# Attention loop with one normalised tile of h per iteration; k's weights over two queues and in halves; v's first product with its low weights last

## The chip, the cores and the metric

The kernel runs on one core of one Trainium2 chip. The metric is the device time of one execution in microseconds (us); of several executions the median is given. One execution was also recorded by the hardware profiler. Its rows are called the profile or the trace here, and times inside it count from the start of the recorded span.

## The reference

The input x is 2048 tokens by 512 channels in float32. First comes attention with a learned feature map, then an MLP that mixes tokens:

```python
h  = x + A(_layernorm(x))
h2 = h + B(_layernorm(h))
# A, for 32 heads of width 16:
q, k, v = split(x @ wqkv)
pq, pk  = q @ w_phi, k @ w_phi                       # per head
phi_q = concat([softmax(pq), softmax(-pq)])          # likewise phi_k
kv, z = phi_k^T v, sum over tokens of phi_k
o  = (phi_q kv) / (phi_q . z + 1e-6);   A = o @ wo
# B, over the token axis, 2048 -> 1792 -> 2048:
u  = gelu(h^T w1 + b1);   B = (u w2 + b2)^T
```

## The kernel before

The 2048 tokens are 16 tiles of 128. Products run on TensorE in a float32 format that takes 128 columns of weights at a time; to keep precision, an operand is split into a high part (a rounded copy, made by ScalarE) and a low part (the difference, made by VectorE or GpSimd). `mm3` (lines 63 to 67) makes of each product three: high by high (L65), high by low (L66), low by high (L67). `split` (L58) makes the two parts.

The engines are called as in the profile: PE (TensorE), PEld (its weight load), ACT (ScalarE), DVE (VectorE), POOL (GpSimd), SP (SyncE, which here only issues DMAs). Each takes its instructions in the order written.

**Start (lines 223 to 362).** Nine products of `ones` (L291 to L293) keep PE at work while the first weights arrive. The transposed weights come in chunks of 128 rows by 512 columns (`load_w`, L228): chunks 4 to 7 are k's, 8 to 11 v's, 0 to 3 q's. All chunks are issued by SP, in the order of the lines 235 to 252, mixed with the tiles of x. Each chunk is centred (`center`, L257: on DVE with a sum, a small multiply and an add of the mean; or on ACT with two passes), folded with the feature map or transposed into PSUM (`fold`, L269), copied out as high weights (`hi_w`, L281) and subtracted to low weights (`lo_w`, L287). For each tile t of x, `split_x` (L109) makes X[t] in two parts, the high one on ACT (L60), the low one on POOL (L61). `proj` (L122) multiplies X[t] with weights; with `by_part` its products stand in an order that lets k's first product begin before all weights are there. From line 294 to line 356 the order of PE, DVE, ACT and POOL is written out by hand; what follows until line 422 (the rest of k, v, and some tiles of q) is ordered by a scheduler. v's first product `v0` (L335) writes into a PSUM buffer of the pool `ps_v` (two buffers), which the folds of chunks 10 and 11 hold until `lo_w` has read them.

**Attention loop (lines 423 to 704).** Again the order on PE, DVE, ACT and POOL is written out by hand. Iteration `it` (L648) works on several tiles at once:

- POOL: `s_pq(it+1)` scales the query features (L465), `s_ez(it+3)` multiplies by z (L447), `s_rstd(it-3)` makes the reciprocal deviation r2 by a power (L590) and multiplies it into the mean (L591), and the low part of the normalised tile is made by L61. In the first iterations `negate` (L160) stands among them.
- PE: `s_num` (L551, even iterations, for two tiles), `q_mm` as long as there are tiles of q, `fills` (L642, up to two tiles of the MLP's first product, L65 to L67 into `pu`), `s_wo(it-2)` (L564, into `po`) and `s_tr(it)` (transposes, L532). `s_num` and `s_tr` share the one PSUM buffer `tn`.
- ACT: copies out of `tn` (`pht`, L534; `oh`, L557), the exponentials (L176), the moments of a tile of h (L585 to L587), the normalised tile `hn` (L595) and its high part (L60), and the high part `whi` of the MLP weights (L614).
- DVE: the denominators (L456 to L462), sums (L221), `ol` (L562), the low part `wlo` of the MLP weights (L606, queued in `LATER` and written by `flush`, L603), and `s_h` (L575), which adds x to the attention's output and frees `po` (one buffer) for the next `s_wo`.

A tile of h thus goes through: `s_wo` and `s_h` in iteration t+2; moments and `s_rstd` in t+3; `s_hn` (L593). In the kernel before, `s_hn` runs only in even iterations, for two tiles: tile it-4 near the beginning (L663), tile it-3 at the end (L697), right behind its own `s_rstd`. The first product of the MLP takes tile it-5 in iteration it (L645).

**MLP (from line 715).** The rest of the first product, gelu, and the second product in a seven-product scheme. The change leaves these lines as they are.

Of the kernel before, what the change touches and what calls it, by code (L numbers as in the profile page):

```python
# [12 lines left out]
ALU = mybir.AluOpType  # L13
# [23 lines left out]
def block_kernel(ctx: ExitStack, tc: tile.TileContext, x, xT, wT, phic, wo, w1, b1, w2, b2,  # L37
# [13 lines left out]
    eps2 = cst.tile([P, 1], F32, name="eps2")  # L51
    r2 = cst.tile([P, NT], F32, name="r2")
    cst.tile([P, 80], F32, name="pad")
    nc.vector.memset(ones, 1.0)
    nc.vector.memset(mhalf, -0.5)
    nc.vector.memset(eps2, EPS * EPS)

# [61 lines left out]
        nc.vector.tensor_scalar(ve, st[:, 1:2], 1.0 / D, EPS, op0=ALU.mult, op1=ALU.add)  # L119
        nc.gpsimd.tensor_tensor(r1[:, t:t + 1], ve, mhalf[:, :1], op=ALU.pow)  # L120

    def proj(t, wh, wl, pool, name, by_part=False):  # L122
        o = pool.tile([P, D], F32, name=name, tag=name)
        if by_part:
            half, whole = [slice(0, D // 2), slice(D // 2, D)], slice(0, D)
            turn = [(0, wh, half[0]), (0, wh, half[1]), (1, wh, whole), (0, wl, half[0]), (0, wl, half[1])]
            for i, (a, w, cols) in enumerate(turn):
                for kt in range(KD):
                    nc.tensor.matmul(o[:, cols], X[t][:, a, kt, :], w[:, kt, cols], start=i == 0 and kt == 0,
                                     stop=i >= 3 and kt == KD - 1, skip_group_check=True)  # L130
            return o
        for kt in range(KD):
            mm3(o, X[t][:, 0, kt, :], X[t][:, 1, kt, :], wh[:, kt, :], wl[:, kt, :],
                kt == 0, kt == KD - 1)
        return o
# [87 lines left out]
    with tc.tile_pool(name="prep", bufs=1) as prep:  # L223
        pc = prep.tile([P, 72], F32, name="pc")
        ph = prep.tile([P, 4, P], F32, name="ph")
        WR = {}

        def load_w(c):  # L228
            if c % 2 == 0:
                pair = big.tile([P, 2, D], F32, name="wraw2", tag="big")  # L230
                WR[c], WR[c + 1] = pair[:, 0], pair[:, 1]
            nc.sync.dma_start(WR[c], wT[c * P:(c + 1) * P, :])

        nc.scalar.dma_start(pc, phic)
        for c in range(4, 8):
            load_w(c)
        xr = {0: load_x(0), 1: load_x(1)}
        nc.sync.dma_start(ident, ident_in)
        for c in range(8, 12):
            load_w(c)  # L240
        xr[2] = load_x(2)
        load_h(0)
        load_h(1)
        xr[3] = load_x(3)
        for c in range(4):
            load_w(c)
        load_h(2)
        xr[4] = load_x(4)
        load_h(3)
        nc.sync.dma_start(mask, kvmask)  # L250
        nc.sync.dma_start(b1s, b1)
        nc.sync.dma_start(b2s, b2)

        FO = {}
        HL = {0: (wqh, wql), 1: (wkh, wkl), 2: (wvh, wvl)}

        def center(c, vector):  # L257

            mu = prep.tile([P, 1], F32, name="mu", bufs=3)
            if vector:  # L260
                nc.vector.reduce_sum(mu, WR[c], axis=AX.X)
                nc.vector.tensor_scalar_mul(mu, mu, -1.0 / D)
                nc.vector.tensor_scalar(WR[c], WR[c], mu, None, op0=ALU.add)
            else:
                junk = prep.tile([P, D], F32, name="junk")
                nc.scalar.activation(junk, WR[c], AF.Copy, scale=-1.0 / D, accum_out=mu)
                nc.scalar.activation(WR[c], WR[c], AF.Identity, bias=mu)

        def fold(c, pool, name):  # L269
            FO[c] = pool.tile([P, KD, P], F32, name=name, tag=name)  # L270
            for kt in range(KD):
                if c < 8:
                    nc.tensor.matmul(FO[c][:, kt, :], WR[c][:, kt * P:(kt + 1) * P], ph[:, c % 4, :],
                                     start=True, stop=True)
                else:
                    nc.tensor.transpose(FO[c][:, kt, :], WR[c][:, kt * P:(kt + 1) * P], ident)

        def parts(c):
            return [w[:, :, c % 4 * P:(c % 4 + 1) * P] for w in HL[c // 4]]

        def hi_w(c, vector=False):  # L281
            if vector:
                nc.vector.tensor_copy(parts(c)[0], FO[c])
            else:
                nc.scalar.activation(parts(c)[0], FO[c], AF.Copy)

        def lo_w(c):  # L287
            hi, lo = parts(c)
            nc.vector.tensor_sub(lo, FO[c], hi)

        warm = ps_k.tile([P, P], F32, name="pk_ps", tag="pk_ps")  # L291
        for _ in range(WARM):
            nc.tensor.matmul(warm, ones, ones, start=True, stop=True)  # L293
        with tc.manual_schedule(engines={ET.PE, ET.DVE, ET.Activation, ET.Pool}):

            nc.gpsimd.tensor_mul(ph.rearrange("p c (a f) -> p c a f", f=DH),
                                 pc[:, 0:64].rearrange("p (c f) -> p c f", f=DH).unsqueeze(2).to_broadcast([P, 4, 8, DH]),
                                 pc[:, 64:72].unsqueeze(1).unsqueeze(3).to_broadcast([P, 4, 8, DH]))
            center(4, True)
            center(5, False)  # L300
            fold(4, ps_q, "pu")
            center(6, True)
            fold(5, ps_q, "pu")
            center(7, False)
            fold(6, ps_v, "pv")
            fold(7, ps_v, "pv")
            hi_w(4, True)
            hi_w(5, True)
            hi_w(6, True)
            split_x(0, xr[0])  # L310
            hi_w(7)
            for c in range(4, 8):
                lo_w(c)
            split_x(1, xr[1])
            k0 = proj(0, wkh, wkl, ps_k, "pk_ps", True)
            center(8, True)
            for c in range(9, 12):
                center(c, False)
            k1 = proj(1, wkh, wkl, ps_k, "pk_ps")
            for c in range(8, 12):  # L320
                fold(c, *((ps_q, "pu"), (ps_v, "pv"))[c // 10])
            k_ops(0, k0)
            split_x(2, xr[2])
            k_ops(1, k1)
            stats_x(0)
            k2 = proj(2, wkh, wkl, ps_k, "pk_ps")
            for c in range(8, 12):
                hi_w(c)
            for c in range(8, 12):
                lo_w(c)  # L330
            stats_x(1)
            exps(0, PK[0])
            split_x(3, xr[3])
            split_x(4, xr[4])
            v0 = proj(0, wvh, wvl, ps_v, "pv")  # L335
            k_ops(2, k2)
            stats_x(2)
            k3 = proj(3, wkh, wkl, ps_k, "pk_ps")
            k_norm(0)
            center(0, True)  # L340
            v_out(0, v0)
# [12 lines left out]
            lo_w(0)  # L354
            lo_w(1)
            center(3, False)
        stats_x(3)
        exps(3, PK[3])
        for c in range(2, 4):
            fold(c, ps_q, "pu")  # L360
            hi_w(c)
            lo_w(c)
# [225 lines left out]

    def s_rstd(t):
        nc.gpsimd.tensor_tensor(r2[:, t:t + 1], VE[t][:, 0:1], mhalf[:, :1], op=ALU.pow)  # L590
        nc.gpsimd.tensor_mul(VE[t][:, 1:2], VE[t][:, 1:2], r2[:, t:t + 1])  # L591

    def s_hn(t):  # L593
        hn = ak.tile([P, D], F32, name="hn")
        nc.scalar.activation(hn, HT[t], AF.Identity, scale=r2[:, t:t + 1], bias=VE[t][:, 1:2])  # L595
        HN[t] = big.tile([P, 2, D], F32R, name="hs", tag="big")
        split(HN[t][:, 0], HN[t][:, 1], hn, nc.gpsimd)
# [47 lines left out]
        if FN[0] <= it - LAG:  # L645
            fill(0, ps_f)

    for it in range(NT + 3):  # L648
        even = it % 2 == 0
        if 0 <= it + 1 < NT:  # L650
            s_pq(it + 1)
# [3 lines left out]
        if it == 1:  # L655
            run(q_logits(0))
            q_mm()
            s_tr(1)
        if it > 1 and even:
            if it <= NT:  # L660
                s_num(it // 2 - 1)
            if it >= 4:
                s_hn(it - 4)  # L663
        den = s_den(it + 2) if it + 2 < NT else []
        if it > 1 and even and it <= NT:
            ol = s_ol(it // 2 - 1)
# [8 lines left out]
        fills(it)  # L675
        q_exp(0)
        logits = q_logits(1)
        if it >= 3 and even:
            s_moments(it - 3)
        if it > 1 and even and it - 2 < NT:  # L680
            s_wo(it - 2)
# [1 line left out]
            s_tr(it)  # L683
        if it > 1 and not even and it - 2 < NT:
            s_wo(it - 2)
        if it >= 3 and not even:
            s_moments(it - 3)
        if it >= 3:
            s_rstd(it - 3)
        run(logits + (q_sums(0) if it > 0 else []), den)  # L690
        flush()
        if 0 <= it - 2 < NT:
            s_h(it - 2)
        if it > 0:
            negate()
        if it >= 3 and even:
            s_hn(it - 3)  # L697
        for p in range(2):
            if it >= LAG - 3 + p and FL[p] <= FN[p] + 2 * (FN[p] > 0):
                fill_load(p)  # L700
# [259 lines left out]
```

## Time and profile before

| what | value |
|---|---|
| time, median of 3 runs | 528.55 us (527.94 to 528.89) |
| the profiled execution's own time | 527.88 us |
| its span | 526.1 us |
| mean granted TensorE clock | 0.999 |
| busy: PE, DVE, ACT, POOL | 516.9, 394.0, 277.7, 245.2 us |

The span is what the instructions cover; the execution takes 1.78 us more. The rows that follow in the prediction are of three kinds. A timeline row gives start, duration, engine, line, operation and tiles; in brackets behind it stands how long the engine was idle before it and who ended that. A group row (of the costliest groups) gives all instructions of one line and shape: busy time, mean of one in ns, and the idle time before them with its releaser. A row of the windows gives, for a stretch of time, the busy time of each engine with the number of its instructions. The end of a matmul is modelled, and neighbours overlap in the pipeline, so distances between starts say more than durations: undisturbed, one matmul of 512 columns starts every 0.23 us.

### The profile page before, as it was taken

The page shows a single profiled execution, that of the slowest core. Times are in us where ns is not written, and L with a number is a line of the kernel's source. Part 1 is how long each engine was busy: PE and PEld are TensorE (multiplying, and loading weights), DVE is VectorE, ACT ScalarE, POOL GpSimd, SP SyncE. Part 2 cuts the span into 40 slices and gives each one's busy share as a digit, 9 for nine tenths or more (in the row PEclk, how much of TensorE's full clock was granted, in tenths as well). Part 3 has the DMA queues.
Part 4 walks back from the last instruction along what each step waited for, and adds up shares of the span by engine and source line. Part 5 has one row for each costly group of instructions (what it writes and reads, how often), then busy time and mean ns, then how long its engine had stood idle before and what let it go on. Part 6 is the DMA issues. An engine that isn't in the chain of part 4 may idle for free.

```text
span 526.1 us, 8910 instructions
## 1 busy us (share of the span) xinstructions
PE 516.9 (98%) x3379; PEld 436.5 (83%) x3379; DVE 394.0 (75%) x681; ACT 277.7 (53%) x480; POOL 245.2 (47%) x204
## 2 busy tenths in 40 slices
PE   9999999999999979999999999999999999999997
PEld 8888888887877757777788888888889999999997
DVE  6893999976899989874426423824869889888985
ACT  6999843534247676557757422625553424444430
POOL 2589699985999988897425000000002122211210
PEclk9999999999999999999999999999999999999999
DMA  8634210020122233334234345532114686667733
GB/s 307 205 120 121 83 40 21 1 87 17 56 86 80 82 103 118 104 119 130 91 101 120 92 143 169 175 104 82 60 61 109 161 191 150 137 153 190 162 44 78
DMA packets 36298, 58.52 MB, mean 111 GB/s; under 512 B 3744, under 2 KB 19360, under 8 KB 36256
## 3 DMA queue, kind: packets, MB, share of 16 engines
q1 hardware_dynamic: 31936, 51.37, 30.4%
q0 software_dynamic: 4032, 6.42, 8.8%
q8 instruction: 26, 0.43, 0.3%
q10 hardware_dynamic: 288, 0.17, 0.1%
q14 instruction: 16, 0.13, 0.1%
HBM read 46.81 MB, written 11.14 MB: 110 GB/s over the span
## 4 chain that ended last, share of the span: by engine, by line
PE 82%; POOL 12%; DVE 3%; ACT 2%; issue 0%; POOLq 0%; ACTq 0%
PE py L822 11%; PE pu L65 11%; PE pu L66 10%; PE pu L67 10%; PE py L826 10%; PE py L823 6%; POOL ez L447 4%; POOL eq L465 3%; PE pv L66 3%; PE pv L67 3%; PE pv L65 3%; PE pk_ps L65 2%; PE pk_ps L66 2%; PE pk_ps L67 2%; POOL hs L61 2%; PE kvp L212 2%
## 5 line engine op out<-in xcount | busy, mean ns | idle before, releaser
L606 DVE TENSOR_TENSOR wlo<-wraw,whi 128x512 fp32r<-128x512 f32 x56 | 50.9, 912 | 56.2 <-ACT whi L614 56.0
L65 PE MATMUL pu<-hs,whi 128*128 128x512 f32 x224 | 87.2, 395 | 0.0
L66 PE MATMUL pu<-hs,whi 128*128 128x512 f32 x224 | 87.1, 389 | 0.0
L67 PE MATMUL pu<-hs,wlo 128*128 128x512 f32 x224 | 87.1, 390 | 0.0
L881 POOL DMA_DIRECT2D out<-ot x7 | 6.2, 889 | 157.3 <-DVE ot L877 157.3
L795 ACT ACTIVATE whi<-wraw 128x1792 fp32r<-128x1792 f32 x28 | 47.5, 1701 | 46.6 <-PE py L822 20.6
L804 DVE TENSOR_TENSOR wlo<-wraw,whi 128x1792 fp32r<-128x1792 f32 x28 | 56.5, 2022 | 12.5 <-PE py L823 8.9
L822 PE MATMUL py<-uf,whi 128*128 128x512 f32 x175 | 63.4, 399 | 0.0
L614 ACT ACTIVATE whi<-wraw 128x512 fp32r<-128x512 f32 x56 | 34.9, 626 | 50.3 <-PE pu L66 46.0
L65 PEld LDWEIGHTS pu<-hs,whi 128*128 128x128 f32 x224 | 42.1, 188 | 10.8 <-issue 2.5
L67 PEld LDWEIGHTS pu<-hs,wlo 128*128 128x128 f32 x224 | 42.1, 188 | 9.0 <-DVE wlo L606 0.4
L823 PE MATMUL py<-uf,wlo 128*128 128x256 f32 x175 | 49.2, 281 | 0.0
L66 PEld LDWEIGHTS pu<-hs,whi 128*128 128x128 f32 x224 | 42.1, 188 | 8.5
L447 POOL TENSOR_TENSOR ez<-eq,zB 128x1024 f32<-128x1024 f32 x16 | 40.6, 2539 | 4.4 <-ACT zB L494 4.4
L826 PE MATMUL py<-uf,whi 128*128 128x256 f32 x210 | 39.0, 283 | 0.0
L822 PEld LDWEIGHTS py<-uf,whi 128*128 128x128 f32 x175 | 33.0, 188 | 6.8
L200 POOL TENSOR_TENSOR pk<-pk,sk 128x1024 f32<-128x1024 f32 x16 | 31.0, 1940 | 7.6 <-DVE sk L199 5.0
L826 PEld LDWEIGHTS py<-uf,whi 128*128 128x128 f32 x210 | 32.4, 189 | 1.4
L823 PEld LDWEIGHTS py<-uf,wlo 128*128 128x128 f32 x175 | 33.1, 189 | 0.0
L465 POOL TENSOR_TENSOR eq<-eq,w 128x1024 f32<-128x1024 f32 x16 | 31.9, 1996 | 1.2 <-DVE w L462 1.2
L204 POOL TENSOR_TENSOR zacc<-zacc,pk 128x1024 f32<-128x1024 f32 x13 | 31.2, 2402 | 0.5
L61 POOL TENSOR_TENSOR hs<-hn,hs 128x512 fp32r<-128x512 f32 x16 | 21.4, 1340 | 17.9 <-ACT hs L60 17.9
(179 smaller groups left out, 1329.2 us busy)
## 6 DMA issues: line engine op xcount, KB each, us to landing
wraw<-in_w SPq DMA_DIRECT2D x56, 256.0 KB, 2.8
wraw<-in_w SPq DMA_DIRECT2D x28, 512.0 KB, 4.1
xraw<-in_xT SPq DMA_DIRECT2D x16, 256.0 KB, 2.9
xh<-in_x SPq DMA_DIRECT2D x16, 256.0 KB, 2.6
h<-in_x SPq DMA_DIRECT2D x16, 256.0 KB, 2.7
out<-h SPq DMA_DIRECT2D x16, 256.0 KB, 3.0
out<-ot POOLq DMA_DIRECT2D x14, 256.0 KB, 4.5
wraw<-in_wT SPq DMA_DIRECT2D x12, 256.0 KB, 4.9
```

The costliest lines, as they stand in the source:

```text
L65: nc.tensor.matmul(o, ah, bh, start=first, stop=False)
L66: nc.tensor.matmul(o, ah, bl, start=False, stop=False)
L67: nc.tensor.matmul(o, al, bh, start=False, stop=last)
L447: nc.gpsimd.tensor_mul(EZ[t], EQ[t], zB)
L465: nc.gpsimd.tensor_mul(heads(EQ[t]), heads(EQ[t]), W[t].rearrange("p g c h -> p (g c h)").unsqueeze(2).to_broadcast([P, 2 * H, DH]))
L606: LO.append(nc.vector.tensor_sub(wl_, raw, wh_).ins)
L614: nc.scalar.activation(wh_, raw, AF.Copy)
L795: nc.scalar.activation(WH[g], RAW[g], AF.Copy)
L804: nc.vector.tensor_sub(wl_, RAW[g], WH[g])
L822: nc.tensor.matmul(o, a[0], b, start=start, stop=stop, skip_group_check=True)
L823: nc.tensor.matmul(o[:, 0], a[1], b[:, 0], start=False, stop=stop, skip_group_check=True)
L826: nc.tensor.matmul(o[:, half], a[x], b[:, y], start=start and first and i == 0, stop=stop and i == 2, skip_group_check=True)
```

## The change

Three groups of edits. (1) At the start, `ones` is set by POOL; chunks 5 and 7 are issued by ACT's queue instead of SP's; chunks 4 and 7 are centred in two halves of 256 columns, and chunk 7's high weights are copied in two halves. (2) v's low weights are made in the order 10, 11, 8, 9, and v0 multiplies with all high weights first and with the low weights in its last four products. (3) In the attention loop, `s_hn(it-4)` runs once in every iteration, behind the exponentials and ahead of the moments; the loop has one iteration more; r2 is multiplied into the mean by ACT ahead of `hn` and no longer by POOL; and where logits are still made in the iteration, `s_h` stands ahead of `flush`.

```diff
-    nc.vector.memset(ones, 1.0)
+    nc.gpsimd.memset(ones, 1.0)
...
-    def proj(t, wh, wl, pool, name, by_part=False):
+    def proj(t, wh, wl, pool, name, by_part=False, low_last=False):
...
+            if low_last:
+                turn = [(0, wh, whole), (1, wh, whole), (0, wl, whole)]
...
-            nc.sync.dma_start(WR[c], wT[c * P:(c + 1) * P, :])
+            (nc.scalar if c in (5, 7) else nc.sync).dma_start(WR[c], wT[c * P:(c + 1) * P, :])
...
-        def center(c, vector):
+        def center(c, vector, parts=1):
...
-                nc.vector.tensor_scalar(WR[c], WR[c], mu, None, op0=ALU.add)
+                for part in range(parts):
+                    cols = slice(part * D // parts, (part + 1) * D // parts)
+                    nc.vector.tensor_scalar(WR[c][:, cols], WR[c][:, cols], mu, None, op0=ALU.add)
...
-        def hi_w(c, vector=False):
+        def hi_w(c, vector=False, parts_of=1):
...
-                nc.scalar.activation(parts(c)[0], FO[c], AF.Copy)
+                for k in range(0, KD, KD // parts_of):
+                    kts = slice(k, k + KD // parts_of)
+                    nc.scalar.activation(parts(c)[0][:, kts], FO[c][:, kts], AF.Copy)
...
-            center(4, True)
+            center(4, True, 2)
-            center(7, False)
+            center(7, False, 2)
-            hi_w(7)
+            hi_w(7, parts_of=2)
...
-            for c in range(8, 12):
+            for c in (10, 11, 8, 9):
                 lo_w(c)
...
-            v0 = proj(0, wvh, wvl, ps_v, "pv")
+            v0 = proj(0, wvh, wvl, ps_v, "pv", low_last=True)
...
     def s_rstd(t):
         nc.gpsimd.tensor_tensor(r2[:, t:t + 1], VE[t][:, 0:1], mhalf[:, :1], op=ALU.pow)
-        nc.gpsimd.tensor_mul(VE[t][:, 1:2], VE[t][:, 1:2], r2[:, t:t + 1])
     def s_hn(t):
+        nc.scalar.activation(VE[t][:, 1:2], VE[t][:, 1:2], AF.Copy, scale=r2[:, t:t + 1])
...
-    for it in range(NT + 3):
+    for it in range(NT + 4):
...
-        if it > 1 and even:
-            if it <= NT:
-                s_num(it // 2 - 1)
-            if it >= 4:
-                s_hn(it - 4)
+        if it > 1 and even and it <= NT:
+            s_num(it // 2 - 1)
...
         logits = q_logits(1)
-        if it >= 3 and even:
+        if it >= 4 and even:
+            s_hn(it - 4)
+        if 3 <= it < NT + 3 and even:
             s_moments(it - 3)
...
-        if it >= 3 and not even:
+        if it >= 4 and not even:
+            s_hn(it - 4)
+        if 3 <= it < NT + 3 and not even:
             s_moments(it - 3)
-        if it >= 3:
+        if 3 <= it < NT + 3:
             s_rstd(it - 3)
         run(logits + (q_sums(0) if it > 0 else []), den)
-        flush()
+        if it > 0:
+            negate()
+        if not logits:
+            flush()
         if 0 <= it - 2 < NT:
             s_h(it - 2)
-        if it > 0:
-            negate()
-        if it >= 3 and even:
-            s_hn(it - 3)
+        flush()
```

More of the change, by code (lines that the diff above doesn't have):

```diff
@@ L120, in stats_x @@
         nc.gpsimd.tensor_tensor(r1[:, t:t + 1], ve, mhalf[:, :1], op=ALU.pow)
-    def proj(t, wh, wl, pool, name, by_part=False):
+    def proj(t, wh, wl, pool, name, by_part=False, low_last=False):
         o = pool.tile([P, D], F32, name=name, tag=name)
-        if by_part:
+        if by_part or low_last:
             half, whole = [slice(0, D // 2), slice(D // 2, D)], slice(0, D)
             turn = [(0, wh, half[0]), (0, wh, half[1]), (1, wh, whole), (0, wl, half[0]), (0, wl, half[1])]
+            if low_last:
+                turn = [(0, wh, whole), (1, wh, whole), (0, wl, whole)]
             for i, (a, w, cols) in enumerate(turn):
@@ L129, in proj @@
                     nc.tensor.matmul(o[:, cols], X[t][:, a, kt, :], w[:, kt, cols], start=i == 0 and kt == 0,
-                                     stop=i >= 3 and kt == KD - 1, skip_group_check=True)
+                                     stop=w is wl and kt == KD - 1, skip_group_check=True)
             return o
@@ L266, in center @@
                 nc.scalar.activation(junk, WR[c], AF.Copy, scale=-1.0 / D, accum_out=mu)
-                nc.scalar.activation(WR[c], WR[c], AF.Identity, bias=mu)
+                for part in range(parts):
+                    cols = slice(part * D // parts, (part + 1) * D // parts)
+                    nc.scalar.activation(WR[c][:, cols], WR[c][:, cols], AF.Identity, bias=mu)
         def fold(c, pool, name):
```

## The prediction

> **What bounds the kernel now.** I read the busy times first, then who ends PE's waits, then the timeline of PE, POOL, ACT and DVE around these waits, and the groups of POOL's instructions in the same stretch.
>
> ```profile
> PE 516.9 (98%) x3379; PEld 436.5 (83%) x3379; DVE 394.0 (75%) x681; ACT 277.7 (53%) x480; POOL 245.2 (47%) x204
> ```
>
> PE is busy for 516.9 of 526.1 us and the change takes no product away. What can be won is PE's lost time, some 9 us, and only the part that the edits touch. Among PE's waits those for `pht`, at `s_num` (L551), are the largest; their rows show where they sit:
>
> ```profile
> 194.84 1.10 PE L551 MATMUL tn<-pht,kvB 64*32 64x256 f32 x32 [2.77 <-ACT pht L534]
> ...
> 208.81 1.10 PE L551 MATMUL tn<-pht,kvB 64*32 64x256 f32 x32
> ...
> 220.84 0.50 PE L65 MATMUL po<-woh,oh 128*128 128x512 f32 x1 [0.76 <-DVE h L579]
> ...
> 238.98 1.10 PE L551 MATMUL tn<-pht,kvB 64*32 64x256 f32 x32 [1.07 <-ACT pht L534]
> ```
>
> `s_num` comes once in two iterations, so the distances between these rows are the time of a pair. From 194.84 to 208.81 it is 13.97 us with no wait of PE: that is PE's own work. From 208.81 to 238.98 are two pairs, 15.08 each. So the loop stalls three times: 2.77 ahead of 194.84, then 1.11 in each of two pairs (the two marked gaps, 0.76 and 1.07, and the refill behind the first). **Together 5.0 us.**
>
> What runs at 15.1 us per pair is POOL:
>
> ```profile
> 202.12 2.40 POOL L447 TENSOR_TENSOR ez<-eq,zB 128x1024 f32<-128x1024 f32 x1
> 204.48 1.00 POOL L590 TENSOR_TENSOR r<-ve,mhalf 128x1 f32<-128x1 f32 x1
> 205.55 0.19 POOL L591 TENSOR_TENSOR ve<-ve,r 128x1 f32<-128x1 f32 x1
> 207.34 1.29 POOL L61 TENSOR_TENSOR hs<-hn,hs 128x512 fp32r<-128x512 f32 x1 [1.59 <-ACT hs L60]
> ```
>
> ```profile
> 205.78 0.82 ACT L595 ACTIVATE hn<-h,ve,r 128x512 f32<-128x512 f32 x1 [2.15 <-POOL ve L591]
> 206.63 0.63 ACT L60 ACTIVATE hs<-hn 128x512 fp32r<-128x512 f32 x1
> ```
>
> POOL makes r and the scaled mean, ACT makes `hn` and its high part from them, and POOL stands idle for 1.59 us until it can subtract. This round trip is there because `s_hn` of the same tile follows `s_rstd` directly. The groups between 196 and 240 us (three pairs) give POOL's work:
>
> ```profile
> L447 POOL TENSOR_TENSOR ez<-eq,zB 128x1024 f32<-128x1024 f32 x6 | 16.2, 2700 | 0.0
> L465 POOL TENSOR_TENSOR eq<-eq,w 128x1024 f32<-128x1024 f32 x6 | 12.1, 2013 | 0.0
> L61 POOL TENSOR_TENSOR hs<-hn,hs 128x512 fp32r<-128x512 f32 x6 | 7.7, 1291 | 4.8 <-ACT hs L60 4.8
> L590 POOL TENSOR_TENSOR r<-ve,mhalf 128x1 f32<-128x1 f32 x6 | 4.2, 698 | 0.0
> ```
>
> Per pair: 16.2, 12.1, 7.7, 4.2, six of L591 at 0.19 (1.1) and 4.8 idle make 46.1, over 3 that is 15.4 by busy times (neighbouring rows overlap a little, hence 15.1 by distances).
>
> **The change, part by part. The loop.** The multiply into the mean leaves POOL for ACT, and the tile that POOL subtracts was started an iteration earlier, so the idle 1.6 goes. What is left for POOL is (16.2 + 12.1 + 7.7 + 4.2)/3 = 13.4 us per pair, 0.6 below PE's 13.97: POOL stops being the bound, PE is late next, and the two gaps of 1.11 go if nothing else is at 15.
>
> The 2.77 us ahead of 194.84 is ACT's:
>
> ```profile
> 188.30 1.03 PE L532 MATMUL tn<-ident,eq 128*128 128x128 f32 x8
> ```
>
> ```profile
> 190.26 0.82 ACT L595 ACTIVATE hn<-h,ve,r 128x512 f32<-128x512 f32 x1 [3.30 <-POOL ve L591]
> ...
> 193.73 1.06 ACT L534 ACTIVATE pht<-tn 128x512 f32<-128x512 f32 x2
> ```
>
> ACT stood 3.30 us at `hn` while the transposes that `pht` copies were done at 189.3. Behind the stuck `hn` were queued its high part, two parts of `whi`, the exponentials and `pht`, and PE waited for the last. In the changed order an odd iteration issues the exponentials and `pht` ahead of the new multiply and `hn`; `pht` then ends near 190.4 (189.3 and its 1.06), before PE asks for it at 194.84 - 2.77 = 192.07. The wait on r now stands at the multiply, with `hn`, its high part, the moments and `whi` queued behind it; r is made one iteration before, so it has long been there.
>
> ACT gets 16 small multiplies, one of them per iteration. The trace has none; the nearest row is a multiply of the same column:
>
> ```profile
> L585 ACT ACTIVATE ve<-ve 128x1 f32<-128x1 f32 x6 | 1.2, 194 | 0.0
> ```
>
> I take 0.2 us. At nothing from below (ACT is at 53%, and its idle time covers it), at 16 x 0.2 = 3.2 us from above if every one were on the path; only the last tile's is, where no later tile hides it, so 0.25 us is in my sum.
>
> Against the gain stands DVE, and that the low part of a tile now comes behind `ez` on POOL:
>
> ```profile
> 202.73 2.33 DVE L606 TENSOR_TENSOR wlo<-wraw,whi 128x512 fp32r<-128x512 f32 x1
> 204.99 0.68 DVE L579 SCALAR_TENSOR_TENSOR h<-po,h 128x512 f32<-128x512 f32 x1
> ...
> 209.31 1.77 DVE L606 TENSOR_TENSOR wlo<-wraw,whi 128x512 fp32r<-128x512 f32 x1
> ...
> 213.38 1.22 DVE L456 TENSOR_REDUCE tz<-ez 128x64 f32<-128x1024 f32 x1 [1.09 <-POOL ez L447]
> ...
> 217.83 2.34 DVE L606 TENSOR_TENSOR wlo<-wraw,whi 128x512 fp32r<-128x512 f32 x1
> 220.09 0.68 DVE L579 SCALAR_TENSOR_TENSOR h<-po,h 128x512 f32<-128x512 f32 x1
> ...
> 256.43 0.68 DVE L606 TENSOR_TENSOR wlo<-wraw,whi 128x512 fp32r<-128x512 f32 x1
> ```
>
> From `h` to `h`, 15.10 us, DVE waited 1.09 for POOL: its work is 14.0 us per pair, level with PE. In it are two `wlo` of 1.77 and 2.34, where one takes 0.68 without POOL beside it (256.43). The `wlo` of 202.73 began beside `ez` and ended at 205.06, 0.54 after `ez` (204.52). So a `wlo` lasts until POOL's instruction is over. It can cost DVE from 0.68 up to 2.40 + 0.54 = 2.94 us, as the new phase has it. Moving `h` ahead of `wlo` acts only in the iterations with logits. I take the measured 14.0, which costs about 0.03 x 5 pairs = 0.2.
>
> ```profile
> 169.32 1.30 POOL L61 TENSOR_TENSOR hs<-hn,hs 128x512 fp32r<-128x512 f32 x1
> 170.57 2.39 POOL L447 TENSOR_TENSOR ez<-eq,zB 128x1024 f32<-128x1024 f32 x1
> ```
>
> ```profile
> 172.75 0.40 PE L66 MATMUL pu<-hs,whi 128*128 128x512 f32 x1
> ```
>
> These two POOL rows change places. The low part then ends where `ez` ended, 172.96, less the 0.65 us of L591 that POOL no longer does before it, so 172.3 against the first need at 172.75: 0.45 to spare. Two iterations on I estimate it 0.3 late, and put 0.3 into the sum. **Loop: -5.0 + 0.3 + 0.2 + 0.25 = -4.2 us.**
>
> **The start.** Rows:
>
> ```profile
> 1.06 3.91 PEld L293 LDWEIGHTS pk_ps<-ones 128*128 128x128 f32 x18 [1.06 <-DVE eps L56]
> 5.18 2.47 PE L273 MATMUL pu<-ph,wraw 128*128 128x128 f32 x16
> 10.13 1.67 PE L129 MATMUL pk_ps<-wkh,xs 128*128 128x256 f32 x8 [0.22 <-ACT wkh L285]
> ```
>
> ```profile
> 3.48 0.69 DVE L261 TENSOR_REDUCE mu<-wraw 128x1 f32<-128x512 f32 x1 [2.45 <-DMA wraw<-in_wT]
> 4.16 0.63 ACT L266 ACTIVATE junk<-wraw 128x512 f32<-128x512 f32 x1 [1.69 <-DMA wraw<-in_wT]
> ```
>
> The first fold starts at 5.18, just behind the `ones` products (4.97). Chunk 4 landed at 3.48 and chunk 5 at 4.16. With a queue each, chunk 5 may come sooner and chunk 4 as much as the distance of the two, 0.68 us, later; half-size adds bring the first fold forward by at most 0.3, and the `ones` products leave only 5.18 - 4.97 = 0.2. Chunk 6 and the tiles of x move up two places in SP's queue; ACT issues two DMAs more before its first work, which its wait of 1.69 us hides (uncovered, chunk 5's centring moves, and with it only the second fold). `ones` by POOL instead of DVE moves products that have that same 0.2 us to spare. I take nothing for all of this (bounds -0.2 and +0.5), and 0.3 for the halves of chunk 7, whose `hi_w` ends the wait of 10.13. The Trainium skill, "DMA: Bandwidth & Descriptors", section "Issuing engines are not separate DMA queues", says that issuing from two engines saves only time of the sequencers; by it too the start of the stream would bring nothing, and no row here shows two queues.
>
> ```profile
> 19.19 1.28 DVE L289 TENSOR_TENSOR wvl<-pv,wvh 128x512 fp32r<-128x512 f32 x2
> ```
>
> ```profile
> 20.53 0.50 PE L66 MATMUL pv<-wvl,xs 128*128 128x512 f32 x1
> ...
> 23.61 0.39 PE L67 MATMUL pk_ps<-wkh,xs 128*128 128x512 f32 x1
> ```
>
> v0 waits for v's low weights and for a buffer of `ps_v`: around 20.5 PE loses 0.6 us. With low weights last, and chunks 10 and 11, which hold the buffer, made first, that goes. 0.3 and 0.6 would make 0.9 to 1.0. But k's fourth product is next:
>
> ```profile
> 21.72 3.82 POOL L61 TENSOR_TENSOR xs<-xraw,xs 128x512 fp32r<-128x512 f32 x3 [0.56 <-ACT xs L60]
> ```
>
> ```profile
> 20.00:48.00 28.00, 27.95 (x138) 23.53 (x139) 21.30 (x38) 27.78 (x63) 24.10 (x19) 1.00 0.39 118
> ```
>
> X[3]'s low part is the first of those three, ends at 21.72 + 3.82/3 = 23.0, and is first read at 23.61. It waits for ACT, which in 20 to 48 us is busy for 27.78 of 28: nothing there moves forward. PE can gain 0.6 before it stands at L67. **Start: -0.65** (bounds 0 and -1.0, and +0.5 if chunk 4 comes late).
>
> **Sum:** -4.2 - 0.65 = -4.85. From the profiled execution's 527.88 us (span 526.1 and 1.78 around it) this gives 523.03. The median of the runs, 528.55, is 0.67 above that execution, so the forecast is 523.7 us.
>
> **The rivals.** (a) *ACT's full stretch eats the start.* All that is won before 20 us is waited off at X[3]; only the loop's 4.2 stays: 528.55 - 4.2 = 524.35. For it speaks 27.78 of 28, against it the slack of 0.6.
>
> (b) *DVE becomes a partial bound.* If both `wlo` of a pair begin beside a fresh `ez`, DVE needs 14.0 + (2.34 - 1.77) = 14.6 us, 0.6 above PE, in some three to four pairs: 2 us given back, 525.7. Against it: a DVE that falls behind POOL meets a shorter rest of `ez` next time.
>
> (c) *Slower: DVE is blocked outright.* POOL now works without a pause, so every `wlo` may be caught by a whole `ez`: 14.0 - 1.77 - 2.34 + 2 x 2.94 = 15.8 us per pair, where 15.1 is the point from which the loop loses. Over the 4.5 pairs from 196 to 260 us this is 4.5 x (15.8 - 13.97) = 8.2 against the 5.0 lost now, +3.2; less 0.65 it comes to about 531. For it speaks that three of the rows above show 1.77 to 2.34; against it, that POOL has 13.4 us of work in 13.97 and that not every one of its instructions is an `ez`. The Trainium skill, "SBUF — State Buffer", section "Who interferes with whom", says that of a VectorE instruction with two SBUF inputs and a GpSimd one that reads SBUF the second to issue is fully blocked. The `wlo` of 202.73 agrees (2.33 against 0.68), and by that rule alone this rival would be the expected one wherever `wlo` issues second.
>
> (d) *The change does not do what it says:* another wait sets the 15.1 us, or r's reader is late in the new order too. Then 528.5.
>
> **How the numbers follow.** The forecast 0.60, (a) 0.12, (b) 0.13, (d) 0.04, (c) 0.11. A difference of 0.2%, about 1.06 us, is what a measurement of this kernel can tell from no change. The forecast, (a) and (b) are faster by more: 0.85; same 0.04; slower 0.11. The range leaves out (c) and (d). Its low end is 523.7 less the 0.75 that I leave in the loop, less 0.35 (1.0 instead of 0.65 at the start) and 0.2 (the first fold earlier), less 0.4 as half the spread of the three runs: 522.0. Its high end is (b) with nothing won at the start (526.35), chunk 4 late by 0.5, and one more low part late by 0.5: 527.4.
>
> **What would show it.** Right: `s_num` at a distance of about 14.0 us throughout the loop; no gap ahead of L551 near 194; no idle of POOL at L61 with ACT's `hs` as the releaser; r's row alone, without L591. At the start no gap near 20.5 and one at L67 of k's fourth product, or none. Wrong: pairs of 15 us or more with DVE's `h` or `ez` as releaser and `wlo` at 2.3 to 2.9; a first fold after 5.3 with chunk 4 as its releaser; PE waiting for the low part of `hs` at L66; a shorter loop whose gain is waited off at the first product of the MLP, where `whi` and `wlo` arrive.

## The result and the profile after

The changed kernel takes 524.58 us (median of 4 runs, 524.36 to 524.80), the kernel before beside it 528.43 us (527.94 to 528.89): a ratio of 0.9927, 95% interval 0.9910 to 0.9944. That is 3.85 us less, where 4.85 were forecast; it lies in the range (522.0 to 527.4). The profiled execution has a span of 523.0 us and an own time of 524.78 us.

The busy times of the changed kernel, and who ended PE's waits (total, times, longest):

```profile
PE 517.2 (99%) x3379; PEld 436.8 (84%) x3379; DVE 386.9 (74%) x681; ACT 282.2 (54%) x498; POOL 240.0 (46%) x189
```

```profile
PE pu L66 <- POOL hs L61: 1.2, 1, 1.2
...
PE pv L279 <- ACT wraw L273: 0.4, 1, 0.4
```

PE's work is the same. The row left out is the wait for `ones` at the very start, 1.0 us, which was 1.1 before. The waits for `pht` and for `h` are gone; two new ones have come, one of 1.2 us for a low part that POOL makes, one of 0.4 us among the folds.

**The loop.** PE's timeline around `s_num` (now L559) and at the new wait:

```profile
189.17 0.50 PE L66 MATMUL pu<-hs,whi 128*128 128x512 f32 x1 [1.18 <-POOL hs L61]
...
194.15 1.09 PE L559 MATMUL tn<-pht,kvB 64*32 64x256 f32 x32
...
208.07 1.09 PE L559 MATMUL tn<-pht,kvB 64*32 64x256 f32 x32
...
221.98 1.09 PE L559 MATMUL tn<-pht,kvB 64*32 64x256 f32 x32
...
235.90 1.09 PE L559 MATMUL tn<-pht,kvB 64*32 64x256 f32 x32
```

A pair of iterations takes 13.91 to 13.92 us each time, where two of the pairs took 15.1 before; that is PE's own pace. The gap of 2.77 us is gone: `s_num` starts at 194.15 instead of 194.84, although a wait of 1.18 us stands ahead of it and PE came into the loop later (below). POOL's groups between 193 and 235 us, three pairs:

```profile
L455 POOL TENSOR_TENSOR ez<-eq,zB 128x1024 f32<-128x1024 f32 x6 | 14.4, 2403 | 0.0
L473 POOL TENSOR_TENSOR eq<-eq,w 128x1024 f32<-128x1024 f32 x6 | 11.9, 1990 | 0.2 <-DVE w L470 0.2
L61 POOL TENSOR_TENSOR hs<-hn,hs 128x512 fp32r<-128x512 f32 x6 | 8.3, 1376 | 2.6 <-ACT hs L60 2.6
L598 POOL TENSOR_TENSOR r<-ve,mhalf 128x1 f32<-128x1 f32 x6 | 4.3, 712 | 0.0
```

Work per pair is (14.4 + 11.9 + 8.3 + 4.3)/3 = 13.0 us, and POOL still waits 0.9 us per pair for ACT. That wait is slack now, since PE waits for nothing in these pairs.

The new wait at 189.17 has its cause in these three POOL rows, which stand one behind the other in iteration 6:

```profile
183.14 1.94 POOL L473 TENSOR_TENSOR eq<-eq,w 128x1024 f32<-128x1024 f32 x1
185.04 2.39 POOL L455 TENSOR_TENSOR ez<-eq,zB 128x1024 f32<-128x1024 f32 x1
187.38 1.74 POOL L61 TENSOR_TENSOR hs<-hn,hs 128x512 fp32r<-128x512 f32 x1
```

The low part waits behind `ez`, and PE asks for it at 189.17 - 1.18 = 187.99. It also takes 1.74 us, where e4 below has 1.28: a `wlo` on DVE runs beside it until 187.98. It is the "two iterations on" of the prediction, where 0.3 us was put.

**The start.** The issues on the two queues (DMA rows give the first issue, the time that all of the row took, and their number), and the centring on ACT:

```profile
0.75 0.86 SPq L234 DMA_DIRECT2D wraw<-in_wT  x2
1.66 0.90 SPq L102 DMA_DIRECT2D xraw<-in_xT  x2
```

```profile
1.19 0.93 ACTq L234 DMA_DIRECT2D wraw<-in_wT  x2
...
4.96 0.63 ACT L270 ACTIVATE junk<-wraw 128x512 f32<-128x512 f32 x1 [1.52 <-DMA wraw<-in_wT]
...
7.64 0.63 ACT L270 ACTIVATE junk<-wraw 128x512 f32<-128x512 f32 x1 [1.19 <-DMA wraw<-in_wT]
```

Chunk 5 is centred at 4.96 (before: 4.16) and chunk 7 at 7.64 (before: 6.49), while chunk 4 came at 3.59 instead of 3.48. Behind chunks 4 and 6, SP goes straight on to two tiles of x at 1.66, which it issued at 2.58 before. PE's rows show what that costs and what the later edits give back:

```profile
8.96 1.16 PE L279 MATMUL pv<-ph,wraw 128*128 128x128 f32 x8 [0.41 <-ACT wraw L273]
9.87 2.56 PE L131 MATMUL pk_ps<-wkh,xs 128*128 128x256 f32 x12
...
23.17 0.39 PE L65 MATMUL pk_ps<-wkh,xs 128*128 128x512 f32 x1
...
23.82 0.50 PE L67 MATMUL pk_ps<-wkh,xs 128*128 128x512 f32 x1
...
48.98 0.30 PE L214 MATMUL kvp<-pk,vs 128*32 128x64 f32 x2
49.21 0.49 PE L65 MATMUL pu<-wqh,xs 128*128 128x512 f32 x1
49.64 0.31 PE L214 MATMUL kvp<-pk,vs 128*32 128x64 f32 x4
```

k's first product starts 0.67 us late (9.87 against 9.20). v0 without its wait brings 0.63 back: at 23.17 PE is level with the kernel before (23.16). Then X[3]'s low part holds it at L67 for a moment (23.82 against 23.61, 0.3 by the next product). At 49.64 four of the `kvp` products stand apart that stood with the others before: the scheduler, given another v0, chose another order for lines that the change doesn't touch (e9 below shows that this goes with v0). By there PE is 0.77 us behind the kernel before, and it enters the loop so (`s_num` of the first pairs starts at 151.90 instead of 151.13).

So in these two traces the loop brings 3.87 us (at the `s_num` near 250 us the changed kernel is 3.10 us ahead) and the start costs 0.77.

### The profile page after: what moved, and what is told of

It reads as the page before. It is cut to its first block, busy times and chain, and to the rows that moved or that the text cites. A ratio compares the mean times of both kernels' runs of the same rounds, so it can differ in the third digit from the quotient of the medians.

```text
span 523.0 us, 8922 instructions
## 1 busy us (share of the span) xinstructions
PE 517.2 (99%) x3379; PEld 436.8 (84%) x3379; DVE 386.9 (74%) x681; ACT 282.2 (54%) x498; POOL 240.0 (46%) x189
## 4 chain that ended last, share of the span: by engine, by line
PE 90%; POOL 6%; DMA 1%; issue 1%; DVE 1%; ACT 0%; ACTq 0%; POOLq 0%
PE pu L65 12%; PE pu L66 12%; PE pu L67 11%; PE py L831 11%; PE py L835 10%; PE py L832 6%; PE pk_ps L67 3%; PE pk_ps L65 3%; PE pk_ps L66 3%; PE pv L66 3%; PE pv L67 3%; PE pv L65 3%; POOL ez L455 2%; POOL eq L473 2%; PE po L65 2%; PE po L67 2%
## 5 line engine op out<-in xcount | busy, mean ns | idle before, releaser
L66 PE MATMUL pu<-hs,whi 128*128 128x512 f32 x224 | 87.6, 391 | 1.2 <-POOL hs L61 1.2
L67 PE MATMUL pu<-hs,wlo 128*128 128x512 f32 x224 | 87.0, 389 | 0.0
L614 DVE TENSOR_TENSOR wlo<-wraw,whi 128x512 fp32r<-128x512 f32 x56 | 44.1, 790 | 53.5 <-ACT whi L622 53.2
L66 PEld LDWEIGHTS pu<-hs,whi 128*128 128x128 f32 x224 | 42.1, 188 | 10.4 <-POOL hs L61 2.2
L67 PEld LDWEIGHTS pu<-hs,wlo 128*128 128x128 f32 x224 | 42.1, 188 | 8.6
L455 POOL TENSOR_TENSOR ez<-eq,zB 128x1024 f32<-128x1024 f32 x16 | 38.3, 2399 | 4.4 <-ACT zB L502 4.4
L542 ACT ACTIVATE pht<-tn 128x512 f32<-128x512 f32 x32 | 17.4, 596 | 30.1 <-PE tn L540 30.1
L61 POOL TENSOR_TENSOR hs<-hn,hs 128x512 fp32r<-128x512 f32 x16 | 21.6, 1352 | 23.7 <-ACT hs L60 23.7
```

What stands on the lines that cost most here:

```text
L66: nc.tensor.matmul(o, ah, bl, start=False, stop=False)
L67: nc.tensor.matmul(o, al, bh, start=False, stop=last)
L455: nc.gpsimd.tensor_mul(EZ[t], EQ[t], zB)
L614: LO.append(nc.vector.tensor_sub(wl_, raw, wh_).ins)
```

## The experiments

Each was timed beside the kernel before, in four sets: e1 to e4, then the repeat, e10, e5 and e6, then e8, e9 and e11, then e12. The kernel before took 527.85, 527.87, 527.56 and 527.96 us in these four sets.

**e1, one queue.**

```diff
-            (nc.scalar if c in (5, 7) else nc.sync).dma_start(WR[c], ...)
+            nc.sync.dma_start(WR[c], ...)
```

> The changed kernel with chunks 5 and 7 back in SP's queue. Theory Q (the second queue makes chunk 7 land later): chunk 7's centring starts near 6.5 us instead of 7.64, the 0.65 us gap among the folds goes, k's first product starts at 9.2 or earlier, and some 0.3 to 0.7 us of the time goes, because X[3]'s low part takes part of it back: 524.0 us. Rival H (the half-size passes on ACT, or its table load, make it late): the first product stays near 9.9 and the time at 524.6.

Measured: 523.52 us (523.39 to 524.00), ratio 0.9914 (0.9900 to 0.9928). All runs lie below all nine of the whole change (524.16 to 524.87). Its trace at the start, ACT and PE:

```profile
4.26 0.63 ACT L270 ACTIVATE junk<-wraw 128x512 f32<-128x512 f32 x1 [1.79 <-DMA wraw<-in_wT]
...
6.37 0.63 ACT L270 ACTIVATE junk<-wraw 128x512 f32<-128x512 f32 x1 [0.63 <-DMA wraw<-in_wT]
```

```profile
8.60 2.57 PE L131 MATMUL pk_ps<-wkh,xs 128*128 128x256 f32 x12
...
22.54 0.50 PE L67 MATMUL pk_ps<-wkh,xs 128*128 128x512 f32 x1
```

k's first product starts 0.60 us earlier than in the kernel before and 1.27 earlier than in the whole change, and X[3] is met 1.07 us earlier than before, at 22.54. Theory Q held, though 0.9 to 1.1 us of the time went instead of its 0.3 to 0.7; H, the halves, fell.

**e2, the loop alone; e3, the start alone.** e2 is the kernel before with the third group of edits alone, e3 the kernel before with the first and second groups alone.

> The kernel before with the third group of edits alone (attention loop). Theory L (the loop brings 3.9 us, the start brings nothing or costs): pairs of 13.9 us and one wait of 1.2 us for the low part near 188; 528.4 - 3.9 = 524.5 us, no slower than the whole change. Rival S (the start brings the forecast 0.65 too, and the loop 3.2): 525.2 us.

> The kernel before with the first and second groups alone (start). Theory L: the loop's num starts some 0.4 to 0.8 us later than before, pairs of 15.1 remain, and the time is 528.4 to 529.2 us. Rival S: 527.8 us, by the forecast's 0.65.

Measured: e2 524.01 us (523.87 to 524.49), ratio 0.9923 (0.9910 to 0.9937); e3 528.16 us (527.78 to 529.43), ratio 1.0007 (0.9998 to 1.0015). The loop alone brings 3.84 us and is as fast as the whole change; the start alone brings nothing that can be told from zero. In e2 `s_num` runs at the same distances (these rows are two pairs apart):

```profile
193.34 1.09 PE L551 MATMUL tn<-pht,kvB 64*32 64x256 f32 x32
...
221.17 1.09 PE L551 MATMUL tn<-pht,kvB 64*32 64x256 f32 x32
```

Theory L held in e2; in e3 the loop begins only 0.15 us later than before (`s_num` at 151.28 against 151.13), not L's 0.4 to 0.8. In the same set e1 stands 0.49 us ahead of e2, with intervals that overlap: that is the most that the start's edits bring once they have one queue.

**The repeat, and e10: the order of the bytes.** e10 is e1 with the loads in another order, all on SP.

```diff
-        for c in range(4, 8):
+        for c in (4, 6, 5):
             load_w(c)
-        xr = {0: load_x(0), 1: load_x(1)}
+        xr = {0: load_x(0)}
+        load_w(7)
+        xr[1] = load_x(1)
```

> The whole change once more, unaltered, so that the others of this call stand beside it on the same chip: 0.9927 of the kernel before, as at first. If chunk 7's late landing is one of many packets sharing the engines, its time may differ from the 7.64 us of the first trace by some tenths.

> The changed kernel with every chunk in SP's queue (as e1), but in the order 4, 6, 5, tile 0 of x, 7, tile 1 of x. Theory O (the second queue cost time because chunk 6 and the tiles of x came ahead of, or level with, chunks 5 and 7): chunk 5 is centred near 4.9 and chunk 7 near 6.8 to 7.2, k's first product starts 0.2 to 0.6 us later than in e1, and the time lies between e1 and the whole change: 523.8 to 524.6 us where the kernel before takes 528. Rival Q (it is the second queue as such): as e1, 523.5 us.

Measured: the repeat 524.44 us (524.16 to 524.87), ratio 0.9931 (0.9919 to 0.9944); e10 524.47 us (524.28 to 524.82), ratio 0.9932 (0.9918 to 0.9945). In e10's trace:

```profile
5.16 0.63 ACT L272 ACTIVATE junk<-wraw 128x512 f32<-128x512 f32 x1 [2.70 <-DMA wraw<-in_wT]
```

```profile
9.60 2.43 PE L131 MATMUL pk_ps<-wkh,xs 128*128 128x256 f32 x12
```

One queue with chunk 6 ahead of 5 and a tile of x ahead of 7 loses what two queues lose, so the order of the bytes is enough to cost this time; that two queues lose by nothing else is not shown. O's time held and Q in e10's sense fell, but chunk 7 was not late here (centred at 6.55, without a wait): with chunk 5 late, k's first product starts 1.00 us behind e1's, where O had 0.2 to 0.6. In the repeat chunk 5 came still later than in the first trace, at 5.54, and PE waited at another fold. Over the five traces of the start with two queues (the whole change twice, e3, e4, e5) chunk 5 is centred at 4.88 to 5.54 and chunk 7 at 6.41 to 7.67; the eight with one queue in the order of before have 4.16 to 4.36 and 6.12 to 6.90. So chunk 5 is late every time, chunk 7 only in some executions.

**e4, the low part ahead of `ez` in iteration 6.**

```diff
-        if it + 3 < NT:
+        if it + 3 < NT and it != 6:
             s_ez(it + 3)
...
         if it >= 4 and even:
             s_hn(it - 4)
+        if it == 6:
+            s_ez(it + 3)
```

> The changed kernel, where in iteration 6 alone z's multiplication s_ez is written behind s_hn, so that POOL makes the low part ahead of it. Theory W (the wait of 1.2 us at L66 stands only because the low part is queued behind ez): the wait goes, no other comes, 523.4 us. Rival (the wait moves on to the next tile, or the later ez delays the denominators and with them PE): 524.3 to 524.6 us.

Measured: 524.77 us (524.63 to 524.82), ratio 0.9936 (0.9923 to 0.9948). Nothing was gained: W fell, and the wait moved on, as the rival had it, but to the next product and by another way than its two. POOL, DVE and PE of e4:

```profile
184.48 1.28 POOL L61 TENSOR_TENSOR hs<-hn,hs 128x512 fp32r<-128x512 f32 x1
185.72 2.40 POOL L455 TENSOR_TENSOR ez<-eq,zB 128x1024 f32<-128x1024 f32 x1
```

```profile
186.04 2.62 DVE L614 TENSOR_TENSOR wlo<-wraw,whi 128x512 fp32r<-128x512 f32 x1
```

```profile
188.72 0.50 PE L67 MATMUL pu<-hs,wlo 128*128 128x512 f32 x1 [1.04 <-DVE wlo L614]
```

The low part is there at 185.76. Now `wlo` begins just behind the moved `ez`, ends at 188.66, 0.54 after `ez`, and PE waits 1.04 us for it at the next product, L67 (and 0.42 us for another at 195.64). In the whole change `wlo` began late in `ez` and took 1.39 us.

**e5, the mean on POOL again; e6, that multiply moved and nothing else.**

```diff
     def s_rstd(t):
         nc.gpsimd.tensor_tensor(r2[:, t:t + 1], VE[t][:, 0:1], mhalf[:, :1], op=ALU.pow)
+        nc.gpsimd.tensor_mul(VE[t][:, 1:2], VE[t][:, 1:2], r2[:, t:t + 1])
     def s_hn(t):
-        nc.scalar.activation(VE[t][:, 1:2], VE[t][:, 1:2], AF.Copy, scale=r2[:, t:t + 1])
```

That is e5, from the whole change; e6 is the reverse of this diff, on the kernel before.

> The changed kernel with r multiplied into the mean on POOL again, as in the kernel before. Theory T (the round trip POOL, ACT, POOL is what bound the loop): POOL has 13.4 + 0.4 = 13.8 us of work per pair, still under PE's 13.9, the pairs stay at 13.9 to 14.0, and only the low part ahead of 188 us comes 0.2 to 0.6 later: as the whole change or up to 0.6 us more. Rival M (the multiply on POOL was what mattered): pairs of 14.3 us or more, 526 us.

> The kernel before with that multiply moved to ACT, in s_hn, and nothing else. Theory T: POOL saves 0.4 us per pair and waits about 0.3 longer for ACT; pairs stay at 15.0 or 15.1 and the stall ahead of num near 194.8 stays; within 0.4 us of the kernel before. Rival M: the pairs come down to 14.6 us or less and 1 us or more of the time goes.

Measured: e5 525.95 us (525.85 to 526.14), ratio 0.9960 (0.9947 to 0.9972); e6 526.74 us, ratio 0.9979 (0.9970 to 0.9989). PE's waits in e5, and e6's `s_num`:

```profile
PE pu L66 <- POOL hs L61: 1.6, 2, 1.4
PE pu L67 <- DVE wlo L614: 0.5, 1, 0.5
```

```profile
223.07 1.10 PE L551 MATMUL tn<-pht,kvB 64*32 64x256 f32 x32
...
238.02 1.10 PE L551 MATMUL tn<-pht,kvB 64*32 64x256 f32 x32 [0.93 <-ACT pht L534]
```

In e5 PE waits neither for `pht` nor for `h`: with the round trip gone POOL can carry the multiply, as T said. But the time is 1.5 us above the repeat's, where T allowed 0.6: the multiply makes the low parts of iterations 5 to 7 later, and `wlo` then meets another POOL instruction. All of it is lost before 209 us; from there e5's pairs take 13.91 us. In e6 a pair still takes 14.95 us: the round trip bounds it. POOL and ACT in e6:

```profile
203.71 1.02 POOL L590 TENSOR_TENSOR r<-ve,mhalf 128x1 f32<-128x1 f32 x1
206.65 1.29 POOL L61 TENSOR_TENSOR hs<-hn,hs 128x512 fp32r<-128x512 f32 x1 [1.92 <-DVE tz L456]
```

```profile
204.76 0.30 ACT L593 ACTIVATE ve<-ve,r 128x1 f32<-128x1 f32 x1 [1.69 <-POOL r L590]
...
205.94 0.63 ACT L60 ACTIVATE hs<-hn 128x512 fp32r<-128x512 f32 x1
```

POOL stands idle from r, which ends at 204.73, until the high part that ACT makes from it ends at 206.57. The row names `tz` of DVE only because that ended last, at 206.66. T was short here too: e6 gains 1.1 us where 0.4 were allowed. M, pairs of 14.6 or less, did not come; yet moving the multiply is worth some 1.1 to 1.5 us by itself, of the 3.84 that the loop brings. e6's trace shows where: about 0.45 us up to the first `s_num` after the gap (194.29 against 194.84, and 0.1 of it from the start), and 0.4 in the next three pairs.

**e8, `wlo` early as well.** e1 with e4's edit and, in iteration 6:

```diff
             den = den[1:]
+            if it == 6:
+                flush()
```

> e1 (all chunks in SP's queue), with e4's edit and one more in iteration 6: the low part wlo of the MLP weights is written right behind ol, ahead of the denominators, so that it issues on DVE before ez does on POOL. Theory B (what moved the wait from L66 to L67 in e4 was that wlo issued behind ez and was blocked until ez ended): wlo takes 0.7 to 1.9 us, both waits near 188 us go, a wait of 0.4 us near 195 may stay; 1 us less than e1: 522.3 to 522.9 us where the kernel before takes 527.9. Rival (wlo is late for another reason, such as its high part on ACT, or the next iteration takes the time back): 523.4 us or more.

Measured: 524.92 us (524.58 to 525.95), ratio 0.9951 (0.9939 to 0.9964): slower than e1. DVE, PE and the windows of e8 (the column behind POOL's is the granted clock):

```profile
191.58 3.55 DVE L614 TENSOR_TENSOR wlo<-wraw,whi 128x512 fp32r<-128x512 f32 x2
```

```profile
195.19 0.50 PE L67 MATMUL pu<-hs,wlo 128*128 128x512 f32 x1 [1.76 <-DVE wlo L614]
```

```profile
188.00:195.00 7.00, 5.43 (x55) 3.70 (x53) 6.83 (x10) 6.00 (x13) 7.00 (x6) 1.00 0.28 85
195.00:201.00 6.00, 5.81 (x18) 4.63 (x19) 5.79 (x14) 2.94 (x7) 6.00 (x4) 0.72 0.51 166
```

Both waits near 188 went, as B said. PE then came sooner to iteration 7, whose two `wlo` were caught by POOL's `ez` and low part, 3.55 us for the two; PE stood 1.76 us, and behind that its clock fell for some 3 us. What was won was lost again, and more: the rival's second way, by which the next iteration takes the time back.

**e9 and e11, the start's other edits undone in e1.** e9 takes out the second group, e11 the halves.

```diff
-            for c in (10, 11, 8, 9):
+            for c in range(8, 12):
                 lo_w(c)
...
-            v0 = proj(0, wvh, wvl, ps_v, "pv", low_last=True)
+            v0 = proj(0, wvh, wvl, ps_v, "pv")
```

```diff
-            center(4, True, 2)
+            center(4, True)
...
-            center(7, False, 2)
+            center(7, False)
...
-            hi_w(7, parts_of=2)
+            hi_w(7)
```

> e1 with the second group undone: v0 takes its low weights in turn and lo_w runs 8 to 11. Theory V (v0's wait costs 0.6 us at 20 us, and its removal is mostly kept): PE loses 0.5 us again near 20.5; 0.2 to 0.6 us more than e1. Rival C (it is taken back at X[3] or by the order that the scheduler then gives the sums kvp near 49 us, which costs about 0.3): as e1 or faster.

> e1 with chunks 4 and 7 centred in whole and chunk 7's high weights copied in whole. Theory V: the wait of 0.2 to 0.3 us in k's first product comes back, 0 to 0.3 us more than e1. Rival C: as e1, because X[3] or the later order takes it back.

Measured: e9 523.72 us (523.36 to 523.87), ratio 0.9922 (0.9909 to 0.9936); e11 523.96 us (523.54 to 524.46), ratio 0.9924 (0.9911 to 0.9938). Neither can be told from e1. In e11 the wait of 0.2 us in k's first product is back; in e9 v0's wait is back, and `kvp` stands as in the kernel before:

```profile
20.42 0.50 PE L66 MATMUL pv<-wvl,xs 128*128 128x512 f32 x1
...
48.71 0.30 PE L214 MATMUL kvp<-pk,vs 128*32 128x64 f32 x2
48.94 0.50 PE L66 MATMUL pu<-wql,xs 128*128 128x512 f32 x1
```

So the other order of `kvp` follows the second group (e11, which keeps that group, has it as e1 does).

The fourteen traces say more of this than the times. From the start of k's first product to the first `s_num` of the loop it is 141.86 to 141.93 us in the four kernels without the second group (before, e2, e6, e9) and 141.97 to 142.07 us in the ten with it. What v0 wins is thus taken back in full before the loop begins, at X[3] and in the other order. What the start is worth shows in when k's first product starts: 9.10 to 9.20 us in three traces of the start of before, 8.60 to 9.13 in four with halves and one queue, 9.59 in e11 without halves, 9.26 to 9.91 in the five with two queues. The spreads of half a microsecond within one start go with the landing of the chunks (in the four, chunk 7 is centred at 6.33 to 6.90), so a single trace prices the start only that well.

**e12, one low part on DVE.**

```diff
-        split(HN[t][:, 0], HN[t][:, 1], hn, nc.gpsimd)
+        split(HN[t][:, 0], HN[t][:, 1], hn, nc.vector if t == 2 else nc.gpsimd)
```

> e1 with the low part of one normalised tile, number 2, subtracted on DVE instead of POOL. Theory B (in iteration 6 the low part stands behind ez on POOL, and wlo may be blocked by whatever POOL runs): the low part is ready by 186 us, the wait at L66 goes, and a wait for wlo of 0 to 0.7 us at L67 takes its place; POOL is 1.3 us earlier in iteration 7, so its two wlo may meet ez at another place. 522.3 to 523.1 us where the kernel before takes 527.9, and e1 523.5. Rival (the iterations 5 to 7 are full on DVE and POOL together, and each relief there comes back as a wait for wlo): 523.4 us or more.

Measured: 523.41 us (523.05 to 524.22), ratio 0.9918 (0.9904 to 0.9932). Of PE's waits in the loop this one is left:

```profile
PE pu L67 <- DVE wlo L614: 0.7, 1, 0.7
```

The wait at L66 went and one of 0.7 us at L67 took its place, as B said, but the time is the rival's (523.4 or more): the gain over e1 is too small to be told from none. e1 and e12 are the fastest versions found, 0.9914 and 0.9918 of the kernel before, about 1 us under the whole change.

## Why the prediction was right, and where it was short

- **POOL's round trip bounds the loop at 15.1 us per pair; without it PE sets 13.97.** Right: 13.91 to 13.92. e6 (14.95 with the round trip kept) and e5 (pairs of 13.91 and no wait for `pht` or `h` with the multiply kept) show that the round trip is the cause, not POOL's load. `s_h` ahead of `flush` was not run by itself; in the trace it stands there only up to 175 us, and from 186 us on `wlo` comes ahead of `h` as before, so it is hardly what shortens the later pairs.
- **The gap of 2.77 us goes because `pht` is issued ahead of `hn`.** It went, in every kernel with the third group.
- **Loop: -5.0 + 0.3 + 0.2 + 0.25.** The 5.0 are gone. The term of 0.3, the low part behind `ez`, was mis-sized: 1.2 us, of which some 0.45 is the low part's own delay beside `wlo` (1.74 us instead of 1.28). PE's wait for it at L66 was one of the prediction's own signs of being wrong; its sign of being right, no idle of POOL at L61, did not come either (0.9 us per pair), but costs PE nothing. The terms for DVE (0.2) and for the last tile (0.25) did not show: from the `s_num` near 250 us to the MLP's second product both kernels take 130.35 us. -4.2 was forecast, -3.84 measured in e2.
- **"I take nothing for all of this", of the queues.** This step failed. The working looked for chunk 4 arriving late; it did not. It named that chunk 6 and the tiles of x move up in SP's queue, and priced this at nothing. In the first trace chunk 5 came 0.8 us and chunk 7 1.15 us later than before, and with one queue about 1.0 us of the time comes back (e1); e10 shows that such an order of the bytes is enough for it. Between 1.5 and 7 us the DMA engines were busy for 0.93 of the time before (310 GB/s) and 0.97 after (317 GB/s), so there was hardly room for one transfer to move up without another moving down.
- **X[3] as the cap, "nothing there moves forward".** Half right. X[3] is met at L67, with a short wait. But in e1 PE met it 1.07 us earlier, past the 0.6 of the prediction: ACT's work did move forward with the start, full as it was (its three high parts of x begin at 20.50 instead of 21.03, and X[3]'s low part on POOL at 21.19 instead of 21.72).
- **Start: -0.65.** Measured with the queue undone: -0.49 (e1 against e2). With it: e3, not different from zero. The second group brings nothing, because X[3] and an order that the scheduler changed further on take it back (e9 and the fourteen traces). The second of these was no term at all in the prediction.
- **Rival (a), 524.35.** The measured 524.58 is nearer to it than to the forecast of 523.7, but not by its way alone: PE waited only some 0.3 us at X[3], and the rest of the start's gain went to the late chunks and to the other order. Of the miss, 0.9 us more at the low part and 0.65 us less at the start stand against 0.45 us of terms that came to nothing; that these cancel in part is luck.
- **Rival (b)/(c), DVE blocked by POOL,** did not bind the whole loop: with POOL ahead, `wlo` mostly fell beside nothing that blocks it. Its group in the changed kernel (193 to 235 us), and in the kernel before (196 to 240 us):

```profile
L614 DVE TENSOR_TENSOR wlo<-wraw,whi 128x512 fp32r<-128x512 f32 x8 | 8.1, 1022 | 0.0
```

```profile
L606 DVE TENSOR_TENSOR wlo<-wraw,whi 128x512 fp32r<-128x512 f32 x6 | 11.0, 1832 | 0.2 <-ACT whi L614 0.2
```

  1.02 us each instead of 1.83: DVE got faster where the prediction feared the opposite. The 14.0 us that the prediction took as DVE's work held such blocked time. Its `wlo` of 256.43 was not without POOL beside it, either:

```profile
256.64 1.63 POOL L61 TENSOR_TENSOR hs<-hn,hs 128x512 fp32r<-128x512 f32 x1 [3.11 <-ACT hs L60]
```

  `wlo` issued first there and took its 0.68 us; it was the low part that took longer. Yet such a block is what holds iterations 6 and 7: e4 and e8 turned the wait for the low part into one for `wlo`. That it would be there in only two iterations was not seen.

What stays open is whether iterations 5 to 7 can be freed from both waits at once; e4, e8 and e12 each freed one.

## What to carry to other kernels

When a pace is set by a loop over engines (POOL to ACT and back), take the tile one iteration earlier: it removes the idle time without removing work, and the engine below it sets the new pace. When the DMA engines are already busy and a queue is split in two, write down the order in which the bytes then go out, and count every transfer that comes ahead of the one that is waited for. When a wait is taken away where two engines are both nearly full, look at what arrives there next: three attempts here turned one wait into another.

## What the runs showed of the hardware

- A `wlo` (two inputs from SBUF, on DVE) that begins behind an `ez` on POOL ends 0.54 to 0.55 us after `ez`, whenever it began: 2.62 us in e4, 1.39 us in the whole change, 0.68 where no POOL instruction was under way. A POOL instruction that issues behind a `wlo` is held in turn: low parts of 1.74 (187.38, whole change) and 1.63 us (256.64, before) instead of 1.28. The Trainium skill, "SBUF — State Buffer", section "Who interferes with whom", calls the port pair that DVE shares with GpSimd an exclusive lock, where issue order decides who blocks; these rows agree. It made the place of one `wlo` worth 1 us of PE time.
- After a stall of 1.76 us (e8, window above) and of 2.77 us (e3) the granted clock was 0.72 between 195 and 201 us, where the kernel before had 1.00 behind the same stall of 2.77 us. The window of e3, then of the kernel before:

```profile
195.00:201.00 6.00, 6.00 (x47) 4.43 (x48) 4.98 (x8) 4.39 (x11) 5.92 (x6) 0.72 0.41 131
```

```profile
195.00:201.00 6.00, 6.00 (x54) 4.58 (x43) 4.93 (x9) 4.39 (x10) 5.92 (x6) 1.00 0.42 133
```

  Some eight matmuls came 0.43 us apart instead of 0.23, about 1.6 us more. So a stall can cost its length once, or nearly double. The Trainium skill, "TensorE: Matmul & The Clock Gate", section "Part 1: The HAM clock gate (the "warmup" mystery)", has a free-running window of about 3.4 us, which agrees with the same stall being punished in one run only. Its table has the throttle come back after at least one idle window of that length; the stalls here were shorter (1.76 and 2.77 us), and the measurement decides. In the four sets all seven runs of the kernel before above 528.5 us show a mean granted clock of 0.992 to 0.994, while none of the nine of the whole change is below 0.999.
